# Expert 0 of a fused attention and mixture-of-experts kernel: two early blocks from the first two pairs of batches instead of three from three, the other two computed singly

## The chip, the cores and the metric

The kernel runs on one core of one Trainium2 chip. The metric is the device time of one execution in microseconds (us), as the median of several runs. TensorE (PE) multiplies, with weight loads (PEld) beside it; VectorE (DVE), ScalarE (ACT) and GpSimd (POOL) do the elementwise work; SyncE (SP) issues the plain DMAs and POOL those with computed addresses. Each engine runs its own queue in order and waits on semaphores.

## The reference

```python
def reference(q, k, v, w_gate, w1, w2):      # q, k, v: (8, 8, 576, 64)
    # attention, windowed: heads 0-3 see the last 32 positions,
    # heads 4-7 every 4th of the last 128
    scores = where(mask, q @ k^T / 8, -1e9)
    attn = softmax(scores) @ v
    x = attn.transpose(0, 2, 1, 3).reshape(4608, 512)
    # 8 experts, each row goes to the one with the largest logit
    logits = x @ w_gate                          # (4608, 8)
    e = argmax(logits); gate = softmax(logits)[e]
    out[row] = gate[row] * (relu(x[row] @ w1[e]) @ w2[e])   # 512 -> 1024 -> 512
```

## The kernel before, in words

**Attention** runs over 36 tiles of 128 rows: four pairs of batches, nine tiles each. A function `step(n)` is a pipeline over the tiles: scores of tile n, transposes of n-1 (`st_trans`, into the one bank T), the product with v of n-2 (`st_av`), transposes of the result of n-3 (`st_xt`), router logits of n-4 (`st_logits`, for three tiles at once). Results go to a table in DRAM (`st_xout`, by POOL). Up to step 34 the engines' order is as written (`MEND = 35`); from step 35 on the compiler's scheduler sets it.

**Routing** of a pair (`route(m)`) is a chain of some 60 small pieces, one or two taken into each step from the list `side`: transposes of the logits (`turn`, L429, out `tl`), maximum, one-hot and running count on DVE, ranks on PE (`rank`, L454 to L458, out `rk`), then nine pairs of marks on DVE (`mark`: `s1` at L474, `b1` at L483, for the first two pairs `b1` on POOL) and nine matmuls on PE (`enter`, L493, out `tb`) that put each row's number in a table of blocks of 128 rows, 40 blocks for each expert. `decode` turns the table into the row list `row_i` (L558 to L565). Rows of one pair can only be gathered when that pair has been routed.

**Experts** are computed in float32 from two rounded parts, so a product takes three matmuls (high with high, high with low, low with high). Each expert has four static blocks (`Static`): the rows are gathered (`fetch_x`), transposed and split (`turn_x` L677, `high_x` L680, `low_x` L684), `layer1` makes for each of eight column groups f twelve matmuls over all blocks' rows together (L714, into `hps`) and two evictions into `h` (L724, L725), `layer2` takes 24 matmuls per block (L744, into `yps`). Single blocks (`Dynamic`) have their rows as the stationary operand instead: 24 matmuls of 512 columns (L794, `hpd`), eight transposes (L810), 24 matmuls (L825, `ypd`). The weights come as eight units of 128x1024 through three buffers `raw` and are split by ACT (L603) and DVE (L604), the first four of expert 0 by ACT (L615) and POOL (L618) inside attention (`split_later`).

**Expert 0 starts early**: `EARLY = 3`. Behind the routing of the third pair (`route(2, early_fetch, early_gates)`) three blocks of its rows are decoded and gathered; `reserve` moves the counter so that later rows go to its fourth block. That block (`rest0`) is a single one, gathered behind the last pair's routing. At the end of attention comes, in this order: the last tiles' work, routing of the last pair, `layer1` of the three blocks, their `layer2`, and `rest0` between them; then expert 1. `blocks_info` (L959 to L992) lists on DVE the blocks left over. The single PSUM bank E is shared by half of the logit transposes, the ranks, the table `tb` and the transposes of gathered rows.

## Time and profile before

| | us |
|---|---|
| median of 3 runs | 689.38 (688.61 to 692.17) |
| the profiled execution | 688.31 |
| its span in the trace | 686.5 |
| scores of the last tile end | 176.8 |
| logits of the last three tiles begin | 192.65 |
| first matmul of expert 0 | 204.80 |
| row list of all blocks written | 215.24 |
| expert 1's own run of matmuls begins | 268.10 |

The profile is one execution. Its times count from the span's start; 1.8 us lie outside the span. It is read here in stages: attention to about 182, its drain and the last routing to 215, expert 0 to 268, and seven more experts to the end. A stage's bound is read from which engine is busy there and, where none is, from which wait ends last.

### The profile page before, as it was taken

Reading aid. Unit: us, or ns where it says so; the run is one execution under the profiler, and the core shown is the slowest. Engines: PE = TensorE matmul, PEld = TensorE weight load, DVE = VectorE, ACT = ScalarE, POOL = GpSimd, SP = SyncE. Lnnn points to the kernel's source line nnn. Section 1 sums busy time; section 2 is a strip of 40 time slices with the busy share of each in tenths; the row PEclk is TensorE's granted clock in tenths of the full one; section 3 lists DMA queues with packets and bytes.
Section 4 is the critical chain, followed back from the end, with each engine's and each line's share of the span. In section 5 each row is a group of like instructions: output and inputs, shape, how many; then the busy total and the mean of one; then the engine's idle time right before and its main releaser. Section 6 shows DMA issues by size and latency. Waiting matters only on the chain. (4 is left out here: it accounts for less than half of the span.)

```text
span 686.5 us, 13176 instructions
## 1 busy us (share of the span) xinstructions
PE 643.9 (94%) x5142; PEld 515.6 (75%) x5142; DVE 395.3 (58%) x831; ACT 329.2 (48%) x644; POOL 264.1 (38%) x304
## 2 busy tenths in 40 slices
PE   7898997999869799999999999999999999999993
PEld 6676775776649578887888888878888887888882
DVE  3675785887858764556356457436645634573410
ACT  2466564667633444455265346436535534562410
POOL 0232365285643146317506612740661273042011
PEclk8999999999978989999999999999999999999997
DMA  9999999984423366476457536646754663664010
GB/s 245 300 303 310 338 305 299 290 261 125 140 78 95 121 198 193 137 239 215 142 196 239 182 131 219 202 133 215 233 155 147 217 215 106 233 213 137 32 46 33
DMA packets 39896, 130.73 MB, mean 190 GB/s; under 512 B 8020, under 2 KB 8824, under 8 KB 39800
## 3 DMA queue, kind: packets, MB, share of 16 engines
q1 hardware_dynamic: 19992, 70.58, 33.0%
q0 software_dynamic: 19840, 59.28, 26.7%
q8 instruction: 41, 0.67, 0.4%
q14 instruction: 23, 0.19, 0.1%
HBM read 110.16 MB, written 20.20 MB: 190 GB/s over the span
## 5 line engine op out<-in xcount | busy, mean ns | idle before, releaser
L604 DVE TENSOR_TENSOR wu<-raw,wu 128x512 fp32r<-128x512 f32 x232 | 149.0, 687 | 88.4 <-ACT wu L603 80.8
L744 PE MATMUL yps<-wu,h 128*128 128x512 f32 x744 | 181.2, 398 | 4.5 <-DVE h L725 4.3
L714 PE MATMUL hps<-x,wu 128*128 128x512 f32 (+1 forms) x768 | 179.7, 390 | 2.8 <-DVE wu L604 1.5
L603 ACT CAST wu<-raw 128x512 fp32r<-128x512 f32 x232 | 131.0, 619 | 88.8 <-DMA raw<-in_w_dram,wi 43.5
L744 PEld LDWEIGHTS yps<-wu,h 128*128 128x128 f32 x744 | 140.7, 191 | 36.5 <-DVE h L725 4.7
L714 PEld LDWEIGHTS hps<-x,wu 128*128 128x128 f32 x768 | 143.4, 190 | 32.1 <-DVE wu L604 1.9
L649 POOL DMA_INDIRECT out_dram<-y,row_i x32 | 35.2, 1099 | 152.5 <-DVE y L648 116.9
L777 POOL DMA_INDIRECT raw<-in_w_dram,wi x56 | 58.5, 1045 | 63.5 <-DVE wu L604 51.0
L725 DVE SCALAR_TENSOR_TENSOR h<-hps,h 128x512 fp32r<-128x512 f32 (+1 forms) x64 | 42.4, 671 | 70.4 <-ACT h L724 52.2
L287 ACT COPY pts<-pt 96x512 f32<-96x512 f32 x72 | 41.9, 582 | 70.5 <-PE pt L282 70.4
L724 ACT ACTIVATE h<-hps 128x512 fp32r<-128x512 f32 (+1 forms) x64 | 36.5, 583 | 78.4 <-PE hps L714 68.2
L261 DVE TENSOR_REDUCE nm<-s 128x4 f32<-128x384 f32 x72 | 39.6, 552 | 41.0 <-PE s L250 40.8
L329 POOL DMA_DIRECT2D x_d<-xs x36 | 20.6, 573 | 107.1 <-DVE xs L317 68.9
L629 POOL DMA_INDIRECT xg<-x_d,row_i x32 | 33.6, 1049 | 56.8 <-PE tpx L768 32.5
L825 PE MATMUL ypd<-wu,hd 128*128 128x512 f32 x192 | 51.1, 404 | 0.0
L282 PE MATMUL pt<-ident,p 128*96 128x128 f32 x288 | 48.1, 291 | 2.3 <-ACT pts L287 1.3
L297 PE MATMUL o<-vr,pts 96*64 96x65 f32 x1152 | 44.3, 230 | 3.2 <-issue 3.1
L297 PEld LDWEIGHTS o<-vr,pts 96*64 96x64 f32 x1152 | 38.7, 142 | 11.3 <-issue 8.9
L794 PE MATMUL hpd<-wu,xd 128*128 128x512 f32 x192 | 45.4, 392 | 0.0
L648 DVE TENSOR_SCALAR y<-yps,gate 128x256 f32<-128x256 f32 x31 | 14.9, 482 | 50.0 <-ACT y L647 47.2
L647 ACT ACTIVATE y<-yps,gate 128x256 f32<-128x256 f32 x31 | 14.6, 472 | 59.3 <-PE yps L744 59.3
L266 DVE TENSOR_TENSOR d<-s,nm 128x384 f32<-128x384 f32 x72 | 40.1, 558 | 4.8
(122 smaller groups left out, 728.4 us busy)
## 6 DMA issues: line engine op xcount, KB each, us to landing
raw<-in_w_dram SPq DMA_DIRECT2D x64, 512.0 KB, 4.3
qkr<-in_qk_dram SPq DMA_DIRECT2D x36, 576.0 KB, 10.4
vr<-in_v_dram SPq DMA_DIRECT2D x36, 390.0 KB, 12.1
x_d<-xs POOLq DMA_DIRECT2D x44, 128.0 KB
x_d<-xs POOLq DMA_DIRECT2D x8, 112.0 KB
raw<-in_w_dram,wi POOLq DMA_INDIRECT x56
x_d<-xs POOLq DMA_DIRECT2D x8, 96.0 KB
x_d<-xs POOLq DMA_DIRECT2D x8, 80.0 KB
```

What stands on the lines that cost most here:

```text
L266: nc.vector.tensor_tensor(st["d", n][:, g], st["s", n][g], st["nm", n][:, g].broadcast_to([P, HP, KB]), op=ALU.subtract,)
L282: nc.tensor.transpose(pt[:KB, h], st["p", n][:, g, h], ident)
L287: nc.scalar.copy(st["pts", n][:, g], st.pop(("pt", n))[:KB])
L297: nc.tensor.matmul(st["o", n][QB * j : QB * (j + 1), g, h], lhsT=pts[:, g, h, QB * j : QB * (j + 1)], rhs=vr[:, n % NRV, a : a + DH + 1], ...
L603: nc.scalar.copy(u[:, 0, sl], raw[:, sl])
L604: nc.vector.tensor_tensor(u[:, 1, sl], raw[:, sl], u[:, 0, sl].bitcast(F32), op=ALU.subtract)
L714: nc.tensor.matmul(hps[:, : self.ns], lhsT=u[:, wpart, fs], rhs=self.x[:, xpart, c, : self.ns], start=(k == 0), stop=(k == 11),)
L725: nc.vector.scalar_tensor_tensor(h[:, 1, :n], hps[:, :n], 0.0, h[:, 0, :n].bitcast(F32), op0=ALU.max, op1=ALU.subtract,)
L744: nc.tensor.matmul(yps, lhsT=self.h[f][:, hpart, ts], rhs=u[:, wpart, fs], start=(k == 0), stop=(k == 23),)
L777: nc.gpsimd.indirect_dma_start(out=raw, out_offset=None, in_=w, in_offset=bass.IndirectOffsetOnAxis(ap=self.wi[:, u : u + 1], axis=0),)
L794: nc.tensor.matmul(hps, lhsT=self.x[:, xpart, c], rhs=u[:, wpart, ns], start=(k == 0), stop=(k == 11),)
L825: nc.tensor.matmul(yps, lhsT=self.h[f // 4][:, hpart, f % 4], rhs=u[:, wpart, fs], start=(k == 0), stop=(k == 23),)
```

## The change

`EARLY` becomes 2 and a new number `EB = 2` counts the early blocks. Expert 0's first two blocks are now filled from the first two pairs and fetched behind the second routing, within attention. Blocks 2 and 3 (`rest0` is a list now) are both computed singly behind the last routing. The first four of eight column groups of the early `layer1` are placed in steps 37 to 40: they use the two score banks S0 and S1 as output and the unused half of the gathered rows' tile `x` for their results. The loads and splits of the first four weight units stand three steps earlier.

```diff
-EARLY = 3
+EARLY = 2
+EB = 2
...
-            e = nc.gpsimd if m < EARLY - 1 else v
+            e = nc.gpsimd if m < EARLY else v
...
-                rest, box["tt"][0:1, 0:1], -1.0, float(3 * P), op0=ALU.mult, op1=ALU.add
+                rest, box["tt"][0:1, 0:1], -1.0, float(EB * P), op0=ALU.mult, op1=ALU.add
...
-        def layer1(self, fs_):
+        def layer1(self, fs_, hps=None, h=None):
+            given = hps, h
...
-    statics = [Static(0, EARLY * S2, 3)] + [Static(e) for e in range(1, NE)]
-    rest0 = Dynamic(fixed=3, units=statics[0].units)
+    statics = [Static(0, EARLY * S2, EB)] + [Static(e) for e in range(1, NE)]
+    rest0 = [Dynamic(fixed=i, units=statics[0].units) for i in range(EB, 4)]
...
     for u in range(4):
-        at(total - 9 + 2 * u, early_load, u)
-        at(total - 7 + 2 * u, early_split, u)
+        at(total - 12 + 2 * u, early_load, u)
+        at(total - 10 + 2 * u, early_split, u)
...
+    def early_layer1(f):
+        n = first.ns
+        hps = psa.tile([P, 512], F32, tag=f"S{f % 2}", name="s")
+        first.layer1([f], hps, first.x[:, :, f, n:])
+
+    for f in range(4):
+        at(total + 1 + f, early_layer1, f)
...
         if i == 0:
-            for f in range(8):
+            for f in range(4, 8):
                 st_.layer1([f])
-                if f % 2:
-                    u = 4 + f // 2
-                    raw = early.pop(u) if u in early else st_.load(u)
-                    st_.units.append(split_unit(1, raw))
-            rest0.fetch_x()
-            units(nx, c, range(4))
-            st_.layer2(0)
-            pull(2)
-            st_.layer2(1)
-            pull(2)
+                raw = early.pop(f) if f in early else st_.load(f)
+                st_.units.append(split_unit(1, raw))
+            for r in rest0:
+                r.fetch_x()
             nx.fetch_x()
             nx.fetch_gates()
-            rest0.prep_x()
-            rest0.layer1()
+            st_.layer2(0)
+            units(nx, c, range(4))
+            pull(1)
+            st_.layer2(1)
+            pull(1)
+            rest0[0].prep_x()
+            rest0[0].layer1()
+            pull(2)
+            nx.prep_x()
+            rest0[0].turn()
+            rest0[1].prep_x()
+            rest0[1].layer1()
             units(nx, a, range(4, 8))
-            pull(1)
-            nx.prep_x()
-            st_.layer2(2)
-            pull(2)
-            rest0.turn()
+            rest0[0].layer2()
+            rest0[1].turn()
             nx.layer1([0])
             pull(1)
-            rest0.layer2()
+            rest0[1].layer2()
+            pull(1)
```

Where instructions stand in their engines' queues, before and after. A row is a line of the kernel, an operation, its output and inputs, and a count; line numbers of the changed kernel are 1 to 16 higher.

PE around the last tile's scores (`s<-qkr`), before:

```order
L454 MATMUL rk<-crun,cc 128x72
L457 MATMUL rk<-oh,ca 128x72
L458 MATMUL rk<-cs,cc 128x72
L232 LDWEIGHTS mk
L232 MATMUL s<-mk 128x384
L232 LDWEIGHTS mk
L232 MATMUL s<-mk 128x384
L250 MATMUL s<-qkr 64x96 x16
L282 MATMUL pt<-ident,p 96x128 x4
L297 MATMUL o<-vr,pts 64x65 x16
L282 MATMUL pt<-ident,p 96x128 x4
L349 MATMUL tp<-ident,xs 128x128 x4
```

The same place of the changed kernel:

```order
L283 MATMUL pt<-ident,p 96x128 x4
L298 MATMUL o<-vr,pts 64x65 x16
L350 MATMUL tp<-ident,xs 128x128 x4
L283 MATMUL pt<-ident,p 96x128 x3
L455 MATMUL rk<-crun,cc 128x72
L458 MATMUL rk<-oh,ca 128x72
L459 MATMUL rk<-cs,cc 128x72
L233 LDWEIGHTS mk
L233 MATMUL s<-mk 128x384
L233 LDWEIGHTS mk
L233 MATMUL s<-mk 128x384
L251 MATMUL s<-qkr 64x96 x16
```

The last tile's scores moved behind four groups that they had stood ahead of: both transposes of tile 34 but one matmul, the product of tile 33 and the transposes of tile 32.

PE from the last logits (`ps_l`) to the ranks and table entries of the last pair, before (`tpx` are transposes of the early blocks' gathered rows, `hps` is layer 1):

```order
L365 MATMUL ps_l<-xt,wgz 32x384 x4
L573 MATMUL tt<-crun,cc 128x8
L429 MATMUL tl<-ident,lgs 128x128 x9
L677 MATMUL tpx<-ident,xg 128x128 x8
L454 MATMUL rk<-crun,cc 128x72
L457 MATMUL rk<-oh,ca 128x72
L458 MATMUL rk<-cs,cc 128x72
L677 MATMUL tpx<-ident,xg 128x128 x4
L714 MATMUL hps<-x,wu 128x384 x3
L493 MATMUL tb<-b_3432,s_3431 128x320
```

The same place of the changed kernel (layer 1 writes the score banks `s` for f = 0 to 3, and `hps` from f = 4):

```order
L366 MATMUL ps_l<-xt,wgz 32x384 x4
L718 MATMUL s<-x,wu 128x256 x12
L463 MATMUL gt<-ident,gate 9x128
L430 MATMUL tl<-ident,lgs 128x128 x3
L718 MATMUL s<-x,wu 128x256 x2
L430 MATMUL tl<-ident,lgs 128x128 x3
L718 MATMUL s<-x,wu 128x256 x10
L430 MATMUL tl<-ident,lgs 128x128 x3
L455 MATMUL rk<-crun,cc 128x72
L718 MATMUL hps<-x,wu 128x256 x10
L458 MATMUL rk<-oh,ca 128x72
L718 MATMUL hps<-x,wu 128x256
```

The three groups of `tpx` went out of this chain; layer 1's matmuls came in between its links. Groups f = 0 and 1 stand ahead of the first row shown, f = 5 and 6 behind the last, among the nine entries `tb`, of which the last six stand with nothing between them.

DVE at the end of `blocks_info` (`tbl`, `tf`), before, where the low part of the last `h` stands, on which layer 2 waits:

```order
L972 SCALAR_TENSOR_TENSOR tbl<-cc,sl_3541,row_i 128x320
L725 SCALAR_TENSOR_TENSOR h<-hps,h 128x384
L980 TENSOR_REDUCE tf_3543<-tbl 128x1
L604 TENSOR_TENSOR wu<-raw,wu 128x512
L982 TENSOR_SCALAR no_3558<-tf_3543,cc 128x7
```

The same place of the changed kernel:

```order
L985 SCALAR_TENSOR_TENSOR tbl<-cc,sl_3591,row_i 128x320
L649 TENSOR_SCALAR y<-yps,gate 128x256
L993 TENSOR_REDUCE tf_3593<-tbl 128x1
L605 TENSOR_TENSOR wu<-raw,wu 128x512
L995 TENSOR_SCALAR no_3608<-tf_3593,cc 128x7
L776 TENSOR_TENSOR xd<-tpx,xd 128x512
```

The last `h` went ahead of this block of 13 instructions; now the eviction `y` of the second early block and then the low part of the first single block's rows (`xd`), on which its layer 1 waits, stand behind it.

## Rows read from the trace of the kernel before

**Rows 1.** The page's first two parts: busy time, share and instructions of each engine; then PE's busy tenths and the granted clock in tenths, in 40 slices of 17.2 us.

```profile
PE 643.9 (94%) x5142; PEld 515.6 (75%) x5142; DVE 395.3 (58%) x831; ACT 329.2 (48%) x644; POOL 264.1 (38%) x304
...
PE   7898997999869799999999999999999999999993
...
PEclk8999999999978989999999999999999999999997
```

**Rows 2.** Busy time by stretch: length, then busy us (and instructions) of PE, PEld, DVE, ACT, POOL, granted clock, DMA share, GB/s.

```profile
182.00:193.40 11.40, 10.54 (x110) 7.03 (x110) 7.97 (x30) 4.33 (x10) 4.96 (x9) 0.85 0.35 114
193.40:204.80 11.40, 6.42 (x33) 4.46 (x29) 6.20 (x27) 3.33 (x7) 5.31 (x6) 0.65 0.27 77
204.80:215.50 10.70, 10.70 (x48) 10.21 (x48) 7.53 (x24) 1.65 (x5) 0.00 (x0) 0.74 0.00 0
...
226.30:238.38 12.08, 7.58 (x32) 5.55 (x32) 9.61 (x27) 5.61 (x11) 0.27 (x1) 0.97 0.33 94
238.38:246.40 8.02, 8.02 (x25) 6.26 (x26) 5.28 (x12) 1.50 (x3) 3.27 (x3) 0.62 0.56 183
...
268.10:300.00 31.90, 31.90 (x147) 26.14 (x146) 17.24 (x28) 16.63 (x31) 8.51 (x9) 1.00 0.51 168
```

**Rows 3.** PE's timeline in the drain: start, time, line, operation, count, in brackets the idle time before it and what ended that.

```profile
175.97 0.89 PE L250 MATMUL s<-qkr 64*64 64x96 f32 x32
176.79 0.64 PE L282 MATMUL pt<-ident,p 128*96 128x128 f32 x4
...
179.30 0.60 PE L349 MATMUL tp<-ident,xs 128*128 128x128 f32 x4
182.00 0.41 PE L493 MATMUL tb<-b,s 128*128 128x320 f32 x1 [2.10 <-DVE s L474]
...
192.65 0.85 PE L365 MATMUL ps_l<-xt,wgz 128*32 128x384 f32 x8 [0.57 <-ACT xt L357]
...
198.62 1.12 PE L677 MATMUL tpx<-ident,xg 128*128 128x128 f32 x4 [1.40 <-DVE x L684]
201.13 0.70 PE L454 MATMUL rk<-crun,cc 128*128 128x72 f32 x2 [1.40 <-DVE x L684]
...
204.80 1.33 PE L714 MATMUL hps<-x,wu 128*128 128x384 f32 x3 [0.68 <-ACT x L680]
```

**Rows 4.** PE's timeline in expert 0, from layer 1 to the start of expert 1, same columns (the last two rows from a second answer of the same view).

```profile
215.88 10.58 PE L714 MATMUL hps<-x,wu 128*128 128x384 f32 x60
...
228.23 5.85 PE L744 MATMUL yps<-wu,h 128*128 128x512 f32 x25 [0.20 <-issue]
238.38 6.78 PE L744 MATMUL yps<-wu,h 128*128 128x512 f32 x16 [4.30 <-DVE h L725]
...
246.37 5.79 PE L794 MATMUL hpd<-wu,xd 128*128 128x512 f32 x24
252.00 0.60 PE L677 MATMUL tpx<-ident,xg 128*128 128x128 f32 x4
252.35 1.87 PE L744 MATMUL yps<-wu,h 128*128 128x512 f32 x7
...
258.68 0.93 PE L810 MATMUL tph<-ident,hs 128*128 128x128 f32 x7
...
262.88 5.38 PE L825 MATMUL ypd<-wu,hd 128*128 128x512 f32 x23
268.10 13.75 PE L714 MATMUL hps<-x,wu 128*128 128x512 f32 x59
```

**Rows 5.** DVE's timeline, same columns: the last running count of the one-hots, the last mark, the table, the row list, the low parts of unit 4, then the last `h` and the block ahead of it.

```profile
198.48 0.30 DVE L512 TENSOR_TENSOR_SCAN cs<-ca,oh 128x72 f32<-128x72 f32 x1
...
209.51 0.38 DVE L483 TENSOR_SCALAR b<-cc,blk 128x320 fp32r<-128x320 f32 x1
212.80 0.49 DVE L543 TENSOR_TENSOR tbl<-tbl,tb 128x320 f32<-128x320 f32 x1 [2.91 <-PE tb L493]
...
214.75 0.49 DVE L565 TENSOR_TENSOR row_i<-scr,none 128x320 int32<-128x320 f32 x1
...
217.57 0.68 DVE L604 TENSOR_TENSOR wu<-raw,wu 128x512 fp32r<-128x512 f32 x1
...
228.77 0.56 DVE L725 SCALAR_TENSOR_TENSOR h<-hps,h 128x384 fp32r<-128x384 f32 x1 [4.49 <-ACT h L724]
...
232.18 0.55 DVE L972 SCALAR_TENSOR_TENSOR tbl<-cc,sl,row_i 128x320 f32<-128x320 f32 x1
...
237.78 0.55 DVE L725 SCALAR_TENSOR_TENSOR h<-hps,h 128x384 fp32r<-128x384 f32 x1
```

**Rows 6.** ACT's timeline: the first cast of unit 7, whose buffer is the one that unit 4 left.

```profile
222.82 1.15 ACT L603 CAST wu<-raw 128x512 fp32r<-128x512 f32 x2 [2.07 <-issue]
```

**Rows 7.** POOL, DVE and PE timelines in attention: POOL's marks of the second pair, its weight splits, a DVE mark beside them and one alone, PE's wait for a mark.

```profile
147.25 3.25 POOL L483 TENSOR_SCALAR b<-cc,blk 128x320 fp32r<-128x320 f32 x3
...
178.14 3.71 POOL L618 TENSOR_TENSOR wu<-raw,wu 128x512 fp32r<-128x512 f32 x3
...
179.64 2.31 DVE L474 TENSOR_SCALAR s<-ca,plc,pay 128x128 fp32r<-128x128 f32 x1
181.98 0.29 DVE L474 TENSOR_SCALAR s<-ca,plc,pay 128x128 fp32r<-128x128 f32 x1
...
150.55 0.41 PE L493 MATMUL tb<-b,s 128*128 128x320 f32 x1 [0.24 <-POOL b L483]
```

More of the change, by code (lines that the diff above doesn't have):

```diff
@@ L701, in unit @@
             self.units.append(split_unit(grp, self.load(u)))
-        def layer1(self, fs_):
+        def layer1(self, fs_, hps=None, h=None):
+            given = hps, h
             for f in fs_:
                 odd = f % 3 == 2
-                hps = pools["ps"].tile(
-                    [P, SLOTS], F32, tag="D" if odd else "A", bufs=1 if odd else 2, name="hps"
-                )
+                hps, h = given
+                if hps is None:
+                    hps = pools["ps"].tile(
+                        [P, SLOTS], F32, tag="D" if odd else "A", bufs=1 if odd else 2, name="hps"
+                    )
                 fs = slice(f * P, (f + 1) * P)
@@ L721, in layer1 @@
                         k += 1
-                h = pools["h"].tile([P, 2, SLOTS], F32R, tag="h", name="h")
+                if h is None:
+                    h = pools["h"].tile([P, 2, SLOTS], F32R, tag="h", name="h")
                 n = self.ns
@@ L853, in fetch @@
             first.fetch_x()
-            for i in range(3):
+            for i in range(EB):
                 at(now[0] + 2 + i, early_x, i)
```

## The prediction, made before the changed kernel ran

> **What bounds the kernel now.** I read the page first: PE is busy 94% of the span, so every stretch in which it is not full, or not at full clock, is what a change in order can win [rows 1]. The slices dip only at 172 to 240 us. The busy times by stretch say why [rows 2]: from 193.4 to 204.8 PE works 6.4 of 11.4 us at a granted clock of 0.65 (the mean of its two levels, 1.2 and 2.4 GHz), to 215.5 it is full at 0.74, from 226.3 it idles 4.5 of 12.1 us, and then it has 0.62 for 8 us. From 268.1 on it is full at 1.00: expert 1 and all behind it are bound by PE, and whatever brings the start of expert 1's run forward brings the end forward as much. So I predict one number, that start, now 268.10 [rows 4].
>
> Two chains lead to it. The first goes from the last tile's scores (175.97 to 176.79) to the last logits at 192.65 [rows 3], and by the last routing to the row list at 214.75 + 0.49 = 215.24 [rows 5]. The second goes from there through the rest of expert 0: 268.10 - 215.24 = 52.9 us.
>
> **The change part by part.**
>
> *Prices.* A layer-1 matmul of 384 columns takes 10.58 / 60 = 0.176 us, one of 512 columns 5.85 / 25 = 0.234 us [rows 4]. One of 256 isn't in the trace. It can't cost more than 0.176; by the line through both it costs 0.176 - 0.058 = 0.118. I take 0.118, since the two rows show hardly any fixed part, and keep 0.176 for the range: for the 60 or so that lie on a path (f = 0 to 3 in the chain, f = 7 behind it), 60 x 0.058 = 3.5 us. The Trainium skill (TensorE: Matmul & The Clock Gate, section LDWEIGHTS) says that a weight load costs its 128 columns / 1.2, 107 ns, whatever streams behind it, so that at 256 columns load and stream are equal; by that page's gap formula the matmul would be 0.109 and the sum 0.5 us better. No row here shows that width.
>
> *A, inside attention (worse by 2.0).* Two groups of transposes of gathered rows move into steps in which PE is full: 252.35 - 252.00 = 0.35 each [rows 4], 0.7. The weight splits on POOL come three steps earlier, and one (3.71 / 3 = 1.24) now stands in POOL's queue ahead of the last three marks of pair 2, for which PE already waited 0.24 [rows 7]: up to 1.24 for PE, since its in-order queue holds the scores behind the table entry. The split's gathers and gates also enter POOL's queue there, but the tiles that wait behind them have three buffers. DVE gets two low parts (about 0.4 each, as under C) and four small ones; it has gaps. I take 2.0, bounds 0.7 and 3.5.
>
> *B, last scores to last logits (better by 0.9).* In the first order shown, PE has both transposes of tile 34, the product of 33 and the transposes of 32 ahead of the last scores: 179.90 - 176.79 = 3.1, all but one transpose, so 3.0 later [rows 3]. What is moved ahead is no longer behind. Of 192.65 - 176.79 = 15.9 us, 2.1 were a wait for a mark that DVE took 2.31 us over instead of 0.29, beside POOL's splits [rows 3, 7]; these splits are gone from there. At 0.85 the clock stood at half for 30% of 11.4 us, 1.7 lost [rows 2]. In between come 16 early matmuls, 16 x 0.118 = 1.9. So 15.9 - 2.1 - 1.7 - 3.0 + 1.9 = 11.0 if all comes at its best, up to 15.9 if the clock and the links between engines don't improve; I take 12.0. Scores + logits: 3.0 - 3.9 = -0.9. With A the last logits begin at 192.65 + 2.0 - 0.9 = 193.8.
>
> *C, last logits to row list (better by 4.1).* The ranks began at 201.13, behind two transposes that passed through the same bank E and waited 1.40 twice, though the running count was there at 198.48 + 0.30 [rows 3, 5]: with the gathered rows prepared earlier, 2.3 less. The third one's low part stood on DVE between the marks, 0.55 as for an `h` of 384 columns [rows 5] and some 0.15 of link: 0.7 less. The last mark ended at 209.89, but the table was added only at 212.80, as PE came late with layer-1 matmuls between entries [rows 5]; in the new order the last six entries stand alone and follow DVE, so some 0.5 is left: 2.4 less. Against it: ten matmuls of f = 3 stand ahead of the third logit transpose, 1.2 less the 0.3 in which DVE reduces, and its low part (0.55 for 384 columns, so 0.4 for 256) ahead of the maximum: 1.3 more. Sum -4.1; the row list is ready at 215.24 + 1.1 - 4.1 = 212.2. At 1.2 GHz the early matmuls would take twice as long: that is a rival below.
>
> *D, row list to expert 1 (better by 1.8).* Work of PE [rows 4]: f = 7, 12 x 0.118 = 1.4; layer 2 of two blocks, 48 x 0.234 = 11.2; two single blocks, each 0.35 of transposes, 5.63 (252.00 - 246.37), eight transposes 1.0, and 5.5 for 24 matmuls (5.22 for 23): 12.5, so 25.0; the transposes for expert 1, 4 x 0.4 = 1.6; its first thirteen matmuls, 3.0. Sum 42.2. The same sum before is 60 x 0.176 + 72 x 0.234 + 12.5 + 1.6 + 3.0 = 44.5; with the idle 4.3 and 3.0 lost to the clock (0.62 is half speed for 76% of 8.02) it makes 51.8 against 52.9, so 1.1 stay unnamed and I keep them. New waits: (1) Unit 7 is loaded when unit 4's buffer is free, 218.25, and cast at 222.82, 7.6 after the row list [rows 5, 6]. Before, 60 matmuls hid that; now only f = 7 and some 25 of layer 2 do, 7.3, and two 0.65 pieces on DVE follow: 1.5 of idle. (2) The first single block's low part is now behind the end of `blocks_info` on DVE, as the last `h` was. That block took 5.6 (232.18 to 237.78) [rows 5] and begins with the first early block's eviction, at row list + 7.6 + 1.3 + 1.4 + 1.2 = 223.7; so it ends at 229.3, and an eviction and two parts of the split follow, by an estimate of 0.7 each from the same 0.55 and a link: 231.4. PE has used up its cover (layer 2, transposes, four high matmuls) at 212.2 + 1.4 + 11.2 + 1.5 + 0.35 + 0.6 + 1.0 = 228.3: 3.1 of idle. (3) Each single block's transposes wait for an eviction, 0.6, of which only the second's is covered: 0.7 in all. (4) An idle of 4.3 brought the half clock and 3.0 lost [rows 2, 4]; for one of 3.1 I take half that, 1.5. Sum 42.2 + 1.1 + 1.5 + 3.1 + 0.7 + 1.5 = 50.1; I add 1.0 for the two places where the three-buffer raw chain and ACT's order meet, which I can't price from a row: 51.1. Before 52.9.
>
> *Sum.* +2.0 - 0.9 - 4.1 - 1.8 = -4.8: expert 1 starts at 263.3. The profiled execution was 688.31, so 683.5; the median lies 1.07 above it: **684.6**.
>
> **The rivals.**
>
> *The clock takes it (slower).* The early matmuls stand in PE's queue between links of the chain. If the drain keeps the clock that it has now (0.65 and 0.74, rows 2), each costs 0.118 more: 60 ahead of the ranks 7.1, 24 among the entries 1.6 where DVE isn't ahead, so the row list comes 8.7 later, at 220.9, and all behind it: 684.6 + 8.7 = 693.3. It decides from a clock of about 0.75 over 182 to the row list; at 0.85 it costs half and the time is no change. For it: chains from DVE still gate PE there. Against it: PE gets 10 us of new work just in the stretch where it idled. The skill's section on HAM oscillation in the same page ties the low clock to idle gaps, which is what the row for 193.4 shows too. Chance 0.12.
>
> *The gain is given back behind the row list (no change).* If unit 7, the late `xd` and the turns of two single blocks cost what the stall before cost, 4.3 + 3.0, and twice 1.0 more, D is +2.5 and the sum -0.5: 688.9. For it: only 17 us of PE work lie between the routing and the first single block, against 29 before. Also here: early matmuls that are late and thus run behind the routing, the change not doing what it says. Chance 0.30.
>
> *The waits don't come (faster).* Without (1), (2) and (4) D is -7.9 and the sum -10.9; with half of them -7.8: 681.6. Chance 0.13.
>
> *POOL's splits hold DVE in attention (slower).* Eight splits run where DVE has three steps' more to do. The row shows a DVE mark at 2.31 beside them and 0.29 alone [rows 7]. If all eight hold a DVE instruction that PE waits for, 8 x 1.24 = 9.9, less 2.1 that B took out already: 692 or so. Beside that row the skill (SBUF — State Buffer, section on the two sides) calls the port pair of VectorE and GpSimd an exclusive lock for a whole instruction, which speaks against moving splits into a busier stretch; the row agrees in its size. But before, two of eight were seen to hold DVE, and PE waited for one. Chance 0.03.
>
> **How the numbers follow.** The forecast, gains of 3 to 6.5 us, has 0.42. The measurement can tell about 0.5%, 3.4 us, from no change. Faster by more: 0.38 of the forecast and the third rival, 0.51. Within: 0.04 and nearly all of the second, 0.34. Slower by more: the clock, the lock and what I don't see, 0.15. The range of 8 in 10 goes from the third rival's 681.6 less 1.4 to the second's 688.9 plus 1.8, a quarter of the clock's cost: 680.2 to 690.7. Matmuls at 0.176 (3.5 us) lie inside it.
>
> **What would show it.** In the changed profile: the last scores near 181.8 and last logits near 193.8 (A, B); ranks within 6 us of them and the row list near 212 (C); granted clock in 193 to 205 above 0.8; a wait of PE for unit 7 and one of about 3 us for `xd` (D); expert 1's run at 263.3. A row list after 216, or two waits of over 4 us behind it, make it wrong.

## The result: slower, and the profile after

| | us |
|---|---|
| the kernel before, median of 20 runs beside the changed kernel | 688.63 (684.86 to 696.26) |
| the changed kernel, median of 20 runs | 693.61 (687.87 to 699.6) |
| ratio | 1.0057, 95% interval 1.0029 to 1.0085 |
| the changed kernel's profiled execution | 693.03, its span 691.2 |

Forecast was 684.6, in a range of 680.2 to 690.7. The changed kernel is slower by 0.57% (by the ratio, some 3.9 us), and outside the range.

Ratios leave out executions in a slower state, which in one set of runs put the kernel before at 1.0075 (1.0031 to 1.0119) against itself, so the ratios of that set are read against this control.

The spans are read in five stages with marks that both kernels have: the start of the scores of step 28 (the 29th tile), up to which PE's order is the same; the logits of the last three tiles; the end of the row list; the start of expert 1's own run of matmuls; the end.

| us | to step 28 | to last logits | to row list | to expert 1 | to the end |
|---|---|---|---|---|---|
| before | 141.4 | 51.2 | 22.6 | 52.9 | 418.4 |
| changed, by the prediction | 141.4 | 52.3 | 18.5 | 51.1 | 418.4 |
| changed | 142.7 | 59.3 | 17.0 | 53.3 | 418.9 |
| before, on another chip | 137.6 | 51.2 | 20.9 | 49.2 | 422.4 |
| changed, on that chip | 144.7 | 61.2 | 16.9 | 52.1 | 421.2 |

The second stage, end of attention and drain, is 8.1 and 10.0 us longer where 1.1 was forecast. The third is shorter by 5.6 and 4.0, as forecast (4.1). The fourth, forecast 1.8 shorter, is 0.4 and 2.9 longer. The first and the last differ between chips and runs by more than between kernels: over the twenty traces of this case the first goes from 137.6 to 145.2, the last from 417.8 to 424.0. The second stage of the kernel before starts and passes step 34's scores at these marks, 29.7 us apart:

```profile
141.41 0.89 PE L250 MATMUL s<-qkr 64*64 64x96 f32 x32
...
171.13 0.89 PE L250 MATMUL s<-qkr 64*64 64x96 f32 x32
```

The page of the changed kernel, its parts 1 and 2, to be held against [rows 1]:

```profile
PE 647.2 (94%) x5174; PEld 517.2 (75%) x5174; DVE 394.4 (57%) x833; ACT 330.8 (48%) x648; POOL 263.8 (38%) x304
...
PE   7989998998798799999999999999999999999993
...
PEclk8999999999998899999999999999999999999997
```

Busy shares are as before; where PE's slices dipped at 11, 12 and 14 (8, 6 and 7), they now dip less, at 10, 11, 13 and 14 (8, 7, 8 and 7). The busy times of the middle three stages and the way to expert 1, split where the low part of `xd` comes, answer to [rows 2] (same columns):

```profile
142.65:190.39 47.74, 39.71 (x641) 30.52 (x640) 32.71 (x86) 28.25 (x60) 33.73 (x41) 0.93 0.57 178
190.39:201.97 11.58, 11.58 (x159) 9.53 (x158) 10.08 (x37) 6.30 (x14) 4.33 (x8) 1.00 0.22 70
201.97:218.97 17.00, 14.27 (x97) 11.35 (x96) 12.27 (x49) 3.80 (x12) 0.00 (x0) 0.97 0.01 1
218.97:240.66 21.69, 17.07 (x68) 13.80 (x68) 18.80 (x57) 10.41 (x21) 14.55 (x14) 0.81 0.59 195
240.66:272.26 31.60, 31.29 (x143) 24.97 (x144) 14.35 (x24) 12.32 (x24) 13.12 (x14) 0.93 0.46 146
```

PE idles 8.0 us between step 28 and the last scores. From these to the last logits it is full at full clock: the drain is what the change meant it to be. From 218.97 on the clock falls to 0.81. PE's timeline says what PE waited for; it answers to [rows 3, 4, 7]:

```profile
142.65 0.89 PE L251 MATMUL s<-qkr 64*64 64x96 f32 x32
...
159.74 0.28 PE L463 MATMUL gt<-ident,gate 128*9 128x128 f32 x1 [1.45 <-DVE se L401]
...
165.19 0.39 PE L574 MATMUL tt<-crun,cc 128*128 128x8 f32 x2 [1.69 <-ACT gts L466]
...
172.38 0.66 PE L678 MATMUL tpx<-ident,xg 128*128 128x128 f32 x4
...
180.60 1.12 PE L678 MATMUL tpx<-ident,xg 128*128 128x128 f32 x4 [2.86 <-DVE x L685]
181.65 1.56 PE L251 MATMUL s<-qkr 64*64 64x96 f32 x32
...
190.39 0.89 PE L251 MATMUL s<-qkr 64*64 64x96 f32 x32
191.21 0.31 PE L283 MATMUL pt<-ident,p 128*96 128x128 f32 x1
...
201.97 0.85 PE L366 MATMUL ps_l<-xt,wgz 128*32 128x384 f32 x8
202.76 1.69 PE L718 MATMUL s<-x,wu 128*128 128x256 f32 x12
204.28 0.27 PE L463 MATMUL gt<-ident,gate 128*9 128x128 f32 x1
...
207.47 0.44 PE L455 MATMUL rk<-crun,cc 128*128 128x72 f32 x2 [0.35 <-DVE lt L435]
...
236.51 1.20 PE L799 MATMUL hpd<-wu,xd 128*128 128x512 f32 x4 [1.67 <-ACT xd L775]
240.66 7.04 PE L799 MATMUL hpd<-wu,xd 128*128 128x512 f32 x20 [2.94 <-DVE xd L776]
...
272.26 7.64 PE L718 MATMUL hps<-x,wu 128*128 128x512 f32 x33
```

The gathered rows' transposes went from the drain into the steps, and the second group waited 2.86 us for the first group's low part. ACT's and DVE's timelines show why; the first group's transposes were done at 173.04:

```profile
178.40 0.83 ACT L389 COPY lgs<-ps_l 64x288 f32<-64x288 f32 x2
179.24 0.58 ACT L681 CAST x<-tpx 128x512 fp32r<-128x512 f32 x1
```

```profile
179.85 0.69 DVE L685 TENSOR_TENSOR x<-tpx,x 128x512 fp32r<-128x512 f32 x1 [2.35 <-ACT x L681]
...
215.79 0.37 DVE L484 TENSOR_SCALAR b<-cc,blk 128x320 fp32r<-128x320 f32 x1
216.67 0.49 DVE L544 TENSOR_TENSOR tbl<-tbl,tb 128x320 f32<-128x320 f32 x1 [0.51 <-PE tb L494]
...
218.49 0.48 DVE L566 TENSOR_TENSOR row_i<-scr,none 128x320 int32<-128x320 f32 x1
...
239.93 0.68 DVE L776 TENSOR_TENSOR xd<-tpx,xd 128x512 fp32r<-128x512 f32 x1
```

The cast stands at the end of ACT's next step, 6.2 us after the transposes, and bank E is taken until the low part behind it is done. The table follows the last mark after 0.5 us [rows 5: 2.9], as forecast.

### The profile page after: what moved, and what is told of

The parts are those of the page before. It is cut to its first block, busy times and chain, and to the rows that moved or that the text cites. A ratio compares the mean times of both kernels' runs of the same rounds, so it can differ in the third digit from the quotient of the medians.

```text
span 691.2 us, 13242 instructions
## 1 busy us (share of the span) xinstructions
PE 647.2 (94%) x5174; PEld 517.2 (75%) x5174; DVE 394.4 (57%) x833; ACT 330.8 (48%) x648; POOL 263.8 (38%) x304
## 5 line engine op out<-in xcount | busy, mean ns | idle before, releaser
L718 PE MATMUL hps<-x,wu 128*128 128x512 f32 (+1 forms) x720 | 167.2, 389 | 3.0 <-DVE wu L605 2.5
L749 PE MATMUL yps<-wu,h 128*128 128x512 f32 x696 | 166.3, 393 | 0.0
L718 PEld LDWEIGHTS hps<-x,wu 128*128 128x128 f32 x720 | 132.7, 190 | 32.1 <-DVE wu L605 3.4
L749 PEld LDWEIGHTS yps<-wu,h 128*128 128x128 f32 x696 | 130.1, 188 | 28.9
L650 POOL DMA_INDIRECT out_dram<-y,row_i x32 | 34.5, 1079 | 141.1 <-DVE y L649 116.4
L730 DVE SCALAR_TENSOR_TENSOR h<-hps,h 128x512 fp32r<-128x512 f32 (+1 forms) x60 | 39.3, 669 | 61.5 <-ACT h L729 53.7
L729 ACT ACTIVATE h<-hps 128x512 fp32r<-128x512 f32 (+1 forms) x60 | 33.9, 581 | 68.4 <-PE hps L718 56.0
L799 PE MATMUL hpd<-wu,xd 128*128 128x512 f32 x216 | 53.6, 405 | 4.6 <-DVE xd L776 2.9
L830 PE MATMUL ypd<-wu,hd 128*128 128x512 f32 x216 | 57.6, 404 | 0.3 <-ACT hd L819 0.3
L799 PEld LDWEIGHTS hpd<-wu,xd 128*128 128x128 f32 x216 | 41.8, 195 | 14.9 <-DVE xd L776 3.4
L830 PEld LDWEIGHTS ypd<-wu,hd 128*128 128x128 f32 x216 | 38.3, 189 | 7.5 <-ACT hd L819 0.7
```

The source lines that it names most:

```text
L718: nc.tensor.matmul(hps[:, : self.ns], lhsT=u[:, wpart, fs], rhs=self.x[:, xpart, c, : self.ns], start=(k == 0), stop=(k == 11),)
L749: nc.tensor.matmul(yps, lhsT=self.h[f][:, hpart, ts], rhs=u[:, wpart, fs], start=(k == 0), stop=(k == 23),)
L799: nc.tensor.matmul(hps, lhsT=self.x[:, xpart, c], rhs=u[:, wpart, ns], start=(k == 0), stop=(k == 11),)
L830: nc.tensor.matmul(yps, lhsT=self.h[f // 4][:, hpart, f % 4], rhs=u[:, wpart, fs], start=(k == 0), stop=(k == 23),)
```

## The experiments

Stages are given as in the table above, in us.

**Where attention lost its time: bank E, the fetch, the splits, the order of the last scores.**

The second group of transposes two steps behind the first:

```diff
-                at(now[0] + 2 + i, early_x, i)
+                at(now[0] + 2 + 2 * i, early_x, i)
```

> The changed kernel with the second early block's transposes two steps behind the first's instead of one. Theory E (the shared bank E is what cost attention its time: the second transposes wait a whole step for the low part of the first, 2.86 us in the trace of the changed kernel, and a stretch of half clock of 3.4 us, 1.7 lost, follows): the 2.86 wait is gone or under 0.7 and the half clock at 180.5 with it, and the time is 3 to 5 us below the changed kernel, about 688. Rival P (POOL's weight splits, three steps earlier, hold DVE and POOL in attention): nothing of it is touched, so the same as the changed kernel within 1.5 us. Rival R (what counts is behind the row list): the same too, or the gain before the row list is seen and is lost again behind it.

Ratio 1.0019 (0.9983 to 1.0055). The 2.86 wait is gone, but the first group waits 1.75 us for the logit sums `lt` that held bank E ahead of it, and the stage to the last logits is 60.4, no shorter: who comes to bank E in these steps waits for whoever holds it. The stage settles little, since this trace had a granted clock of 0.87 up to step 34's scores where the changed kernel's had 0.94 (5.2 and 2.3 us lost at most); in time the run is 0.4% below the changed kernel, with intervals that overlap, and theory E's 3 to 5 us are not shown. The wait for `lt` comes and goes (under 0.4 in the changed kernel, 1.83 in the run with the written order below). In this trace DVE stands still for 1.32 us ahead of it while POOL works off the gates' two gathers; whether these hold it wasn't tried.

The evictions in the same step as the transposes, all one step later:

```diff
-                at(now[0] + 2 + i, early_x, i)
+                at(now[0] + 3 + i, early_x, i)
...
         first.turn_x(i)
-        spare.insert(0, (lambda: first.high_x(i), lambda: first.low_x(i)))
+        first.high_x(i)
+        first.low_x(i)
```

> The changed kernel with the transposes of each early block one step later and, in that same step, ACT's and DVE's evictions of them, so that bank E is held for a few instructions and not over a whole step. Theory E (bank E costs attention its time): PE waits for no low part before the last scores (2.86 us in the changed kernel), from step 28's scores to the last logits takes 53 to 56 us (59.3 in the changed kernel, 51.2 before), and the time is 3 to 5 us below the changed kernel, between before and 0.2% above it. Theory W (behind the row list PE waits for DVE's chain to xd, so time won ahead comes back): row list earlier, but the two waits for xd longer than 1.67 and 2.94, and the time within 2 us of the changed kernel.

1.0015 (0.9975 to 1.0055). To the last logits 56.2 instead of 59.3, to expert 1 52.3. Theory E's stage is nearly as expected (53 to 56). Up to step 34's scores, where PE's order is as written, the six runs with evictions in the transposes' own step take 33.6 to 35.5 us, and the six that have them a step later 37.4 to 40.4, and in this run PE no longer waits 2.86 us for a low part. So the time for which the bank is held is what costs, though the transposes also start a step later here. In time the run is 0.4% below the changed kernel, with intervals that overlap. The two waits for `xd` are 1.75 and 2.89, as in the changed kernel, against theory W.

The same, with the gates of the second pair written ahead of the fetch (`then()` behind `gate_out`, early rows again at `now[0] + 2 + i`, which are the same steps as in the run above):

> The run with the parts at once, and in the routing of the second pair the gates' sum, reciprocal and transpose written ahead of the early fetch, whose four decode instructions had stood between. PE's order stays but for these. Theory K (the fetch in the middle of attention costs, as decode delays the gates, on which PE's transposes and, behind ACT's copy, the count wait: 1.30 and 1.69 us, against 0.27 and 1.36 in the kernel before): the first wait falls to 0.3, from step 28's to step 34's scores takes 1 to 2 us less than in the run with the parts at once (35.5), and the time is 1 to 2 us less, which may be below what the interval can tell. Otherwise: the same wait appears at the next reader of bank E, and nothing changes.

PE's wait for the gates fell from 1.30 to 0.26, as theory K had it, and the stage to step 34's scores from 35.5 to 33.6, to the last logits 54.3. The stage doesn't prove it: the three runs with this order have 33.6, 33.6 and 34.5 to step 34, the three without it 34.0, 34.9 and 35.5. Nor does the ratio, 1.0062 (1.0025 to 1.0100).

The early rows' transposes in the drain and no group of layer 1 there:

```diff
-                at(now[0] + 2 + i, early_x, i)
+                at(total + 1 + i, early_x, i)
...
-    for f in range(4):
-        at(total + 1 + f, early_layer1, f)
...
-            for f in range(4, 8):
+            for f in range(8):
```

> The changed kernel with all of early layer 1 behind the drain and the early blocks' transposes moved to the drain as well, as in the kernel before: of the change there remain the two blocks instead of three, their earlier gather, the earlier splits and the two single blocks. Theory E: from step 28 to the last scores takes 35 to 38 us (47.7 changed, 46.5 without drain groups, 34.6 before), and the time is 4 to 6 us below the run without drain groups, so about that of before or 1 to 2 us under it. Rival S (the earlier fetch itself, that is decode on DVE, the count and the gathers on POOL, or the second single block is what costs): 2 us or less below the run without drain groups.

1.0026 (0.9991 to 1.0062). To the last logits 51.6, against 57.1 in the run without drain groups (given below): the rows' passage through E in attention costs 5.5 us, and 5.2 of them lie ahead of step 34's scores (33.6 against 38.8). PE's timeline has these two marks first in the run without drain groups, then here; step 28's scores start at 142.53 and 137.71:

```profile
181.30 0.89 PE L251 MATMUL s<-qkr 64*64 64x96 f32 x32
...
199.64 0.85 PE L366 MATMUL ps_l<-xt,wgz 128*32 128x384 f32 x8
```

```profile
171.32 0.89 PE L251 MATMUL s<-qkr 64*64 64x96 f32 x32
...
189.31 0.85 PE L366 MATMUL ps_l<-xt,wgz 128*32 128x384 f32 x8 [0.24 <-ACT xt L358]
```

The forecast of 35 to 38 us to the last scores was missed by a little (38.4): 2.5 us of the fetch remain, against 49.1 with the splits alone. In time the run is 0.45% below the one without drain groups, 3.1 us, between theory E's 4 to 6 and rival S's 2, with intervals that overlap. Its stages do not say so: the transposes lie behind the last logits here, and expert 1 starts 129.0 us from step 28, against 126.9 in that run.

The kernel before with only the splits earlier, and once more on the control's chip:

```diff
-        at(total - 9 + 2 * u, early_load, u)
-        at(total - 7 + 2 * u, early_split, u)
+        at(total - 12 + 2 * u, early_load, u)
+        at(total - 10 + 2 * u, early_split, u)
```

> The kernel before with one thing changed: loads and splits of the first four units of expert 0 three steps earlier, as in the change. Rival P (splits in a busier stretch): the last tile's scores come 4 us later or more, and the kernel is 3 us slower than before or more. Theory E (bank E and the early rows): within 1.5 us of before, and rather faster, since two DVE marks that stood beside POOL's splits (2.31 and 1.59 us) get free.

> The kernel before with loads and splits three steps earlier, a second time, on the chip of the control: 0.2 to 0.5% faster if the first result (0.4%, interval from 0.8% faster to no change) was real; no change if it was chance.

0.9962 (0.9922 to 1.0003), and 1.0010 (0.9974 to 1.0046) where the control stood at 1.0075. To the last logits 49.1 in both, 2.1 less than before. DVE's mark that took 2.31 us beside POOL's splits [rows 7] takes 0.34 here (its timeline in the first of the two runs, then PE's wait for it in the second, 2.10 before):

```profile
182.93 0.34 DVE L474 TENSOR_SCALAR s<-ca,plc,pay 128x128 fp32r<-128x128 f32 x1
```

```profile
180.69 0.42 PE L493 MATMUL tb<-b,s 128*128 128x320 f32 x1 [0.49 <-DVE s L474]
```

Rival P is out: the earlier splits are a part of the change that pays. They are not free, though. From step 28's to step 34's scores they cost 1.4 us (31.1 instead of 29.7, in all four traces of the kernel before that have them), and behind the last scores they give back 3.5 (13.2 to the last logits instead of 16.7). The cost stands at the first split. In the kernel before two DVE marks take 1.09 us in all; in the changed kernel they take 1.66 beside POOL's split, and PE then waits 0.73 for DVE; it waits as long in the first of the two runs above. The lines are from the kernel before (DVE), from the changed kernel (DVE, POOL, PE) and from that run (PE):

```profile
146.41 1.09 DVE L474 TENSOR_SCALAR s<-ca,plc,pay 128x128 fp32r<-128x128 f32 x2
```

```profile
148.39 1.66 DVE L475 TENSOR_SCALAR s<-ca,plc,pay 128x128 fp32r<-128x128 f32 x2
148.50 1.35 POOL L619 TENSOR_TENSOR wu<-raw,wu 128x512 fp32r<-128x512 f32 x1
152.29 0.32 PE L233 MATMUL s<-mk 128*128 128x384 bf16 x1 [0.73 <-DVE d L267]
```

```profile
153.45 0.32 PE L232 MATMUL s<-mk 128*128 128x384 bf16 x1 [0.73 <-DVE d L266]
```

The written order kept for one more step (`MEND = 36`):

> The changed kernel with the written order of the engines kept for one step more, so that the last tile's scores stand ahead of the groups that the scheduler had put before them. If that place costs (rival O): last scores 3 to 4 us earlier, last logits 2 us earlier or more, and the time 2 us below the changed kernel. If only the order of the same work changes (my reading): last logits within 1 us, the time within 1.5 us of the changed kernel.

1.0137 (1.0055 to 1.0220), from only four runs: slower than before and no faster than the changed kernel, whose interval this one overlaps, so against rival O. The last scores are no earlier (190.7), since the ranks ahead of them now wait for bank E too, 2.97 us, and the stage to the last logits is 63.6, against my reading:

```profile
189.58 0.44 PE L455 MATMUL rk<-crun,cc 128*128 128x72 f32 x2 [2.97 <-DVE x L685]
```

In the changed kernel the ranks do not wait there: the scheduler's order, which looked like a delay of the last scores, seems to have hidden that wait.

**What the groups in the drain are worth.**

> The changed kernel with all eight column groups of the early layer 1 behind the last routing, none in the drain. Theory F (the groups in the drain are what paid, 48 matmuls at 0.14 taken off the path, 6.7 us, but they are missing as fill under the last marks, where a stretch of half clock of 6.8 us from 218 costs 3.4): PE is full from the ranks to the row list, the half clock at 218 is gone or earlier, and the time is 2 to 4 us above the changed kernel. Rival G (the groups slow the routing chain by as much as they save): within 1.5 us of the changed kernel, the row list earlier by 2 us or more.

The changed kernel with all of layer 1 behind the routing (the two edits at `early_layer1` and `range(8)` above): 1.0071 (1.0040 to 1.0102), the same as the changed kernel. To the last logits 2.2 us less, to the row list 1.1 less, to expert 1 only 0.5 more although 48 matmuls of 256 columns are back: PE's two waits for `xd` shrink from 1.67 and 2.94 to 0.68 and 0.92, and the granted clock over this stage rises from 0.88 to 0.96. In the changed kernel the work taken off PE behind the row list had left PE waiting for DVE. Theory G holds there.

> As the run with the parts at once, and no column group of layer 1 in the drain. Theory G (the drain groups buy nothing: they hold the routing chain by about what they take off PE behind it): the same as the run with the parts at once within 1.5 us, its row list 2 to 3 us earlier, its waits for xd shorter by as much. Theory F (they pay 2 to 4 us): slower than that run by so much.

With the evictions mended: 1.0052 (1.0015 to 1.0088) against 1.0015 with the groups. The row list comes 4 us sooner counted from step 28 (69.0 against 73.1), but expert 1's run 2.3 later (127.7 against 125.4). Here the groups seem to pay, some 2 us in the stages of one pair of traces, and theory F is nearer; in time the intervals overlap. If that is so, bank E and the missing cover behind the row list hid a gain from each other; the spread of single traces leaves it open.

**The list of left-over blocks on DVE.** In the changed kernel, and in the kernel before behind `rest0.layer1()`:

```diff
-    dti, dwi = blocks_info(cc[...], DBLK)
-    dyn = [Dynamic(dti[:, i : i + 1], dwi[:, i]) for i in range(DBLK)]
...
             rest0[0].layer1()
+            dti, dwi = blocks_info(cc[...], DBLK)
+            dyn = [Dynamic(dti[:, k : k + 1], dwi[:, k]) for k in range(DBLK)]
```

> The changed kernel with the listing of left-over blocks written behind the first single block's first layer, so that the low part of xd and the last splits stand ahead of those 14 DVE instructions of half a microsecond. Theory D (that block is what xd waits for: 2.94 us, and half clock for 6.8 us after it, 2.3 to 3.4 lost): the wait is under 1 us, expert 1's run starts 3 to 5 us sooner, and the time is 3 to 5 us below the changed kernel, about 688. Rival Q (the chain raw buffer, cast, low part sets the time there anyway): a wait for a weight unit takes its place, and the time is the same within 1.5 us.

> The kernel before with the listing of left-over blocks written behind the single block's first layer, so that it stands behind the last h on DVE. If the list is what PE waited for there (4.30 us, with 3.0 lost to the clock behind it): the wait is gone and expert 1's run starts 4 to 7 us after the row list sooner. Theory X (what is won ahead of expert 1 is kept, PE being the bound from there): 4 to 6 us faster than before. Rival Y (experts 1 to 7 are held nearly as much by their weights' chain, and PE that comes sooner waits for units): 2 us or less faster, with waits of PE for low parts or h at the experts' starts of 5 us or more in all, 2.1 in the kernel before.

The stage does what theory D says. PE's timeline of the first of the two has all 24 matmuls in one piece:

```profile
232.73 5.85 PE L799 MATMUL hpd<-wu,xd 128*128 128x512 f32 x24 [1.36 <-ACT xd L775]
```

From the row list to expert 1 it takes 49.8 instead of 53.3, and 47.2 in the kernel before. The times do not follow: 1.0087 (1.0046 to 1.0127) and 1.0009 (0.9976 to 1.0043). Behind the start of expert 1 PE waits 6.1 and 5.0 us in all in these two traces, 2.1 in the kernel before and 3.0 in the changed one. That fits rivals Q and Y, but the control's rest took 422.4 with 5.3 us of such waits and nothing changed, so these stages don't show it.

**All together, on one chip with a control.**

> The kernel before, unchanged, as the control on this chip. Ratio 1.000 within 0.4%. If chips differ in one stage only (rival C), one of the stages up to step 28's scores, from there to the row list, to expert 1's run, and to the end has another length than in the first trace (141.4, 73.8, 52.9, 418.4) by over 2 us; if not, all are within 1.5.

> The changed kernel, unchanged, on the same chip: 0.3 to 0.9% slower than before. By the reading so far the stages against the control's are: step 28 to last logits 7 to 9 us longer, from there to the row list 5 to 6 shorter, to expert 1's run within 1.5, to the end within 1.5.

> The changed kernel with three places mended: parts at once, gates ahead of the fetch, list of left-over blocks late. Theory X (a start of expert 1 that comes sooner brings the end as much): expert 1's run 4 to 7 us sooner than the control's counted from step 28, the rest within 1 us of it, and 0.5 to 1% faster than before. Rival Y (experts 1 to 7 give it back in waits for late evictions, behind casts that wait for weights): start as under X, the rest 2 us longer or more, waits of PE there of 4 us or more against some 2, and the time 0.3% faster to 0.5% slower.

Medians of 685.65, 694.98 and 683.31 us; ratios 1.0075 (1.0031 to 1.0119), 1.0209 (1.0163 to 1.0256) and 1.0025 (0.9982 to 1.0067). Against the control the changed kernel is 1.3% slower (1.0209 / 1.0075), clear of noise, and the mended one 0.5% faster (1.0025 / 1.0075), with intervals that overlap. Most of these forecasts missed. The control was to stand within 0.4% of itself. The changed kernel's stages were to be 7 to 9 longer, 5 to 6 shorter and then the same, and were 10.0, 4.0 and 2.9. The mended kernel was to start expert 1 by 4 to 7 us sooner than the control, counted from step 28, and did so by 1.1 (120.2 against 121.3); against rival Y, its rest was no longer than the control's (420.8 and 422.4). The stages of the last, in windows cut at the same marks with a cut more at the last scores and at the first matmul on `xd`:

```profile
142.24:180.55 38.31, 34.62 (x594) 26.85 (x593) 28.42 (x75) 25.24 (x54) 30.91 (x37) 0.96 0.68 204
180.55:196.56 16.01, 15.62 (x208) 12.34 (x207) 13.17 (x48) 9.47 (x22) 7.43 (x12) 1.00 0.30 93
196.56:213.50 16.94, 14.18 (x97) 11.25 (x96) 12.32 (x49) 3.71 (x12) 0.00 (x0) 0.99 0.02 8
213.50:229.94 16.44, 15.05 (x65) 11.82 (x65) 13.05 (x40) 9.40 (x21) 12.83 (x12) 0.91 0.73 251
```

and of the control:

```profile
137.58:172.13 34.55, 32.35 (x589) 24.95 (x588) 27.71 (x72) 23.59 (x51) 24.01 (x31) 1.00 0.56 173
172.13:188.81 16.68, 13.41 (x180) 10.11 (x179) 13.89 (x47) 9.03 (x21) 9.98 (x14) 0.90 0.45 143
188.81:209.68 20.87, 15.86 (x84) 13.24 (x84) 13.46 (x50) 4.80 (x12) 5.80 (x6) 0.84 0.18 51
```

Mended, attention to the last scores still takes 3.8 us more than the control, the routing 3.9 less, and from the row list to expert 1 (48.9 and 49.2) it is the same. It is faster where the prediction had put the gain. The kernel before with the earlier splits alone starts expert 1 sooner still on this chip, 118.4 us from step 28.

> The changed kernel with the parts at once and the list of left-over blocks late: both waits that the traces named, 2.86 in attention and 2.94 for xd, taken away together. Theory X: expert 1's run starts 6 to 8 us sooner counted from step 28's scores than in the changed kernel (129.6), and the time is 5 to 7 us below it, 0.3 to 0.5% faster than before. Rival Y: the start is sooner by as much, but the time is at best that of the run with the parts at once, 0.1 to 0.3% above before.

> The kernel before with both edits that touch nothing of the early blocks: splits three steps earlier, and the list of left-over blocks late. Theory X: the sum of the two, 0.8 to 1.2% faster than before. Rival Y: no more than the earlier splits alone, 0.3 to 0.5%.

> The changed kernel with the three places mended, a second time. If the mended change is worth something: 0.2 to 0.8% faster than before, from step 28's scores to the last logits 54 to 55 us again and from there to the row list 17. If it only takes back its own losses: within 0.2% of before.

> The kernel before with earlier splits and the late list, a second time: 0.3 to 0.7% faster than before, from step 28's scores to the last logits 49 us. If it beats the mended change by 0.2% or more, the early blocks of two pairs are not worth their routing, decode and transposes inside attention.

The two mended places without the gates' order gave 1.0059 (1.0024 to 1.0094), although its start of expert 1 (120.9 from step 28) came as early as theory X said: a miss for X. The time is above rival Y's too. All three again, on a further chip: 0.9958 (0.9926 to 0.9989). The kernel before with earlier splits and the late list: 0.9969 (0.9933 to 1.0004), below the 0.8 to 1.2% of theory X, and, beside the mended change, 0.9932 (0.9898 to 0.9965). That kernel, which has none of the change's moved blocks, is faster than the kernel before in the second of these and by 0.3% in the first, whose interval just reaches no change. It stands 0.26% ahead of the mended change beside it, with intervals that overlap: that the moved blocks are worth nothing is likely and not shown.

## Why the prediction was wrong

**A failed: "I take 2.0, bounds 0.7 and 3.5".** The last scores came 14.4 us later, not 5.0; 1.2 of that lies ahead of step 28. To step 34's scores, where the order is still as written, the loss is 9.3 us (39.0 instead of 29.7), above the upper bound. The term priced the transposes as PE work, 0.7, one split at up to 1.24, and the fetch at nothing. The traces give the parts up to this mark. The splits cost 1.4 (31.1 against 29.7, four traces), near their price, though by holding DVE and not in POOL's queue. Fetch, decode, gates and count cost 2.5 (33.6 against 31.1, one pair of traces). The transposes cost 5.2 (38.8 against 33.6, one pair): this is the step that failed, since the term did not ask how long they hold bank E. Half clock behind the waits is in these figures, 2.3 of the 9.3 at most (0.94 over 39.0 us), and A had no term for it.

To the last logits the parts are: earlier splits -2.1 (49.1 against 51.2), fetch +2.5 (51.6 against 49.1), the rows' passage +5.5 (57.1 against 51.6), the groups in the drain +2.2 (59.3 against 57.1). They add up to the 8.1 measured, since they are differences of one row of traces; three traces of the changed kernel's attention spread from 58.3 to 61.2, so the fetch and the groups are not clear of that spread. The row that would have warned stood in C: transposes through E waited 1.40 us twice [rows 3]. The prediction credited that where they left and charged nothing where they went, and there the eviction stands a step away and not next in line.

**B was right in its own size.** From the end of the last scores (191.21) to the last logits took 10.8 us, 12.0 forecast and 11.0 at its best, at a clock of 1.00. The first rival, in which the clock takes the gain in the drain, did not happen.

**C was right** in size: 17.0 us to the row list, 18.5 forecast, with the ranks 5.5 behind the last logits and the table 0.5 behind the last mark, and 16.9 on the other chip. In part that may be luck: its sum has waits alone, while the granted clock over this stage rose from 0.70 to 0.97 in the first pair of traces and to 1.00 on the other chip (0.84 before), and no run parts the two.

**D failed in (2) and (4), by size.** It was to save 1.8 and lost 0.4 and 2.9. Unit 7 cost PE no idle time of its own, (1) forecast 1.5. The waits for `xd` were 4.6 and 4.9, (2) forecast 3.1, and the late list shows that the block ahead of it on DVE is the cause of the second part, as named. The clock was forecast to lose 1.5. At 0.81 over 21.69 us it was at half for 38%, 4.1 at most, and at 0.93 over the next 31.60 for 14%, 2.2 at most. The first of these stretches begins as PE follows the last marks (14.27 busy of 17.00 us): the groups that used to lie between the entries had been spent in the drain. That the clock there hangs on this cover was only argued; in the run without drain groups it fell as well, less in one trace (0.96 over the stage). The second rival had D at +2.5, where 0.4 and 2.9 came; alone it would have given no change. Its +2.5 does not follow from its own terms, though: 7.3 in place of the waits' 6.8, and 2.0 more, make D 53.6, which is +0.7.

**Prices.** The price was right: within a group matmuls of 256 columns start 0.119 us apart (the mean of 81 in the changed kernel's trace), where 0.118 was taken. The first of the group shown above takes 0.22, so that its twelve take (204.28 - 202.76) / 12 = 0.127 on average. The page's formula (the Trainium skill, TensorE: Matmul & The Clock Gate, section Back-to-back issue gap) had given 0.109; the measurement decides. One reading was wrong: PE's slices dip to 7 at 103 to 120 us too [rows 1], not only from 172 to 240, but no term rests on it.

**The fourth rival happened in part.** Earlier splits freed DVE where they had stood, 0.34 us for a mark instead of 2.31, and held it where they went, the 1.4 us under A. What the Trainium skill says of the pair's lock (SBUF — State Buffer, section on the two sides), that the second comer is blocked for the other's whole instruction, agrees with 2.31 against 0.34 in kind. In size, as the prediction had it, it does not: one split takes 1.24, so the mark was held for longer than one. In the changed kernel's trace on the other chip one DVE instruction on a single element took 4.08 us beside three of POOL's splits, and PE waited 2.10 us for a result behind it; the same instruction took 0.15 in the changed kernel's first trace (last line):

```profile
167.14 4.08 DVE L401 SCALAR_TENSOR_TENSOR crun<-rest,crun 1x1 f32<-1x1 f32 x1
167.47 3.73 POOL L619 TENSOR_TENSOR wu<-raw,wu 128x512 fp32r<-128x512 f32 x3
173.62 0.55 PE L430 MATMUL tl<-ident,lgs 128*128 128x128 f32 x3 [2.10 <-DVE lt L435]
...
165.79 0.15 DVE L401 SCALAR_TENSOR_TENSOR crun<-rest,crun 1x1 f32<-1x1 f32 x1
```

To the last logits that trace is 1.9 us longer than the first. Still, in the kernel before the earlier splits gain more than they cost, so nothing here makes them the cause of the loss.

**"Whatever brings the start of expert 1 forward brings the end forward as much"** left something out. Starts from 255.9 to 275.0 us were followed by rests from 417.8 to 424.0, and runs that start sooner by an edit were timed from 0.9% slower to 0.7% faster than before. In all twenty traces the rest is 404.2 to 405.2 us of PE at full clock and 11.6 to 11.9 behind its last matmul; what differs is PE's idle time, 1.2 to 6.1, and half clock, 0 to 3.4 us. The idle time does not go by the start: the kernel before has 2.1 and 5.3 us of it in two traces. What sets it stays open.

## What to carry to other kernels

When instructions that pass through a single buffer are moved, charge the buffer's holding time in the new place, up to the end of the eviction where that stands in its own engine's queue, by the same row from which the old place is credited. Work that covers a wait can be spent once: moved ahead, it leaves the next chain bare, so price the stretch it leaves as well as the one it fills. Before a change of under 1% is explained, run the unchanged kernel as one of the candidates, and read stages with marks that both kernels share.

## What was not expected of the hardware

The same kernel has medians from 683.80 to 691.18 us on the chips of this case, and the twenty traces reach step 28, up to which PE's order is the same, between 137.6 and 145.2 us. The stage behind it repeats to 0.1 us for one order and not for others: 49.0 to 49.1 in all four traces of the kernel before with earlier splits, 51.2, 51.2 and 52.5 in the three without, 58.3 to 61.2 in the three with the changed kernel's attention. So a difference of 2 us between single traces shows little. Nor do times show much more: two measurements gave the changed kernel 1.0057 and, against its control, 1.0133 (1.0209 / 1.0075), and the kernel before with both edits 0.9969 and 0.9932. Most experiments here are decided by a stage and by how often it came out the same.
